# A new order of steps and buffers in an unrolled TensorE-bound kernel (decay attention, then a mixture of attention experts)

## The chip, the cores and the metric

The kernel runs on one core of one Trainium2 chip. The metric is the device time of one execution in microseconds (us). Engine names in the profile: PE is TensorE, PEld its weight loads, DVE is VectorE, ACT is ScalarE, POOL is GpSimd, SP is SyncE, which here only issues DMAs.

## What is computed

Two stages, cut from the reference. B = 4 batches, H = 8 heads, S = 768 tokens, D = 48; then E = 4 experts, Hd = 64, model width 384.

```python
def _attn_ref(r, k, v, w, u):
    state = np.zeros((B, H, D, D))
    for t in range(S):
        kt, vt, rt = k[:, :, t], v[:, :, t], r[:, :, t]
        cur = np.einsum('bhd,bhe->bhde', u[None] * kt, vt)
        y[:, :, t] = np.einsum('bhd,bhde->bhe', rt, state + cur)
        state = w[None, :, :, None] * state + np.einsum('bhd,bhe->bhde', kt, vt)

def _moe_ref(x, w_gate, wq, wk, wv, wo):          # x: (4, 768, 384), K = 2, scale = 1/8
    logits = x @ w_gate
    topk = np.argpartition(-logits, K, axis=-1)[..., :K]
    w = softmax of the two largest logits
    for e in range(E):
        q, k, v = x @ wq[e], x @ wk[e], x @ wv[e]
        a = softmax(causal(scale * (q @ k.transpose(0, 2, 1))))
        ye = a @ v @ wo[e]
        out += (gate weight of e, 0 where e is not in topk) * ye
```

## The kernel before

**The first stage** works on 24 chunks of 128 tokens (n = 0 to 23, six per batch). k and r of a chunk lie in rotating buffers `kdbuf` and `rdbuf` (four each), v in `vhbuf`, and a copy of v with its halves exchanged in `vsbuf`. The steps of a chunk: `load_chunk` and `load_vh` (DMAs on SP's queue), `load_vs`, `a_decay` (k and r times tables of powers of w; on DVE at L512 for the first chunks, on POOL at L514 for the others), `a_ku` (POOL, L521 and L523: the products for the u term), `a_own` (DVE, L530 and L532: their sum, times v), `a_transpose` (PE, L542: four transposes of k, four of r; copied out of PSUM by ACT into `kt`, L550, `rt`, L559, and `rx`, L563; chunk 0 by DVE, L548 and L556), `a_quarters` (PE, L579: scores inside 64 x 64 blocks, then the outer products of k and v, L587, called sums here), `a_mask` (DVE, L596, makes `sm`), `a_sum` (DVE, L635, and POOL, L639: the running state `z`), `a_out` (PE, L612 and L616), `a_add` (DVE, L623, twice: the chunk's x, in `ownv`), `a_xt` (PE, L646, transposes x; ACT, L649, copies its rounded part `xt_hi`) and `a_xl` (DVE, L656, the remainder `xt_lo`).

**The tables** are made once: a DMA brings w (`load_w`, L294 on ACT's queue), a transpose turns it (L297), `powers` builds the powers on DVE, `table` (L423, L425) expands them, L431 transposes them into the one buffer `psb` of two PSUM banks, and `table_out` (ACT, L435) copies them to `tab_k` and `tab_r`. The first `a_decay` steps on DVE read them in `psb`.

**The second stage** works on groups G of three chunks (eight groups, two per batch). Each weight is split in two numbers, hi and lo (`hi_qk` on ACT and `lo_qk` on DVE, L476, make `wqk_hi` and `wqk_lo`; `hi_v` and `lo_v`, L489 and L491, the same for `wv`), and each product is three matmuls. The steps: `m_proj` (PE, L687: q and k), `m_values` (PE, L722: v and the gate's logits), `m_gate` (DVE), `m_scores` (PE, L774 and L775, into `psb`; DVE, L781, mask and maximum; ACT, L783, exp), `m_weigh` (POOL, L796), `m_turn` (PE, L804: transposes; ACT, L808, copies them to `pt`), `m_av` (PE, L824) and `m_out` (PE, L847 to L849, then a copy and the DMA out). `warm_up` (L354) and `keep` (L393) are PE work without a result, put among the first steps.

**The order.** Every step is a generator that stops at places inside it. All of the program is unrolled from one table, ORDER, of 1629 words. A word names a step and its arguments and lets it run to its next stop; the digits behind "/" are the numbers of the rotating buffers that it takes there (PSUM: six of one bank, `ps`, and the one `psb`; in SBUF among others six `pr` and twelve `pt`). Each engine's and each DMA queue's instructions stand in the order in which the words issue them, and the framework puts a semaphore wait wherever an instruction needs another engine's or queue's. So a word that stands elsewhere moves everything that it issues, on every engine.

Of the kernel before, what the change touches and what calls it, by code (L numbers as in the profile page):

```python
# [21 lines left out]
a_decay,1,1 load_uw/2 warm_up a_quarters,0/34 a_quarters,0 a_transpose,1/0 a_mask,0/01 a_decay,2,1 load_uw load_vs,0
load_vs,0 a_transpose,0/0 a_ku,1/0 a_ku,1 a_ku,0/1 a_ku,0 lo_o,1 a_transpose,2/5 a_sum,0/0 a_transpose,1/1
a_transpose,2/0 a_transpose,1/1 load_vs,1 a_transpose,1/11 table_out,0 a_transpose,2/2 a_out,0 a_own,1/01 a_sum,0
a_own,0/0 a_quarters,1/5 a_transpose,2/22 a_sum,0/1 a_ku,2/0 a_decay,3,0 a_sum,1 a_add,0 a_sum,1/2 a_quarters,2/12
a_xt,0/3 keep,0/4 a_transpose,3/4 load_vs,2 hi_v load_vs,2 load_vs,1 a_transpose,3/1 a_xt,0/0 a_ku,2 load_chunk,4
load_qk,1/5 hi_qk,1 load_vh,3 load_chunk,4 load_chunk,5 a_mask,1/23 a_out,1 load_qk,0/2 load_vh,4 load_chunk,5
a_mask,2/01 a_sum,2 a_own,2/0 a_out,2 load_vh,6 load_chunk,6 load_chunk,6 load_vh,5 a_decay,3,1 a_decay,4,0 a_xl,0/0
a_ku,4/1 a_ku,3/0 a_sum,2/0 a_ku,3 a_decay,4,1 a_decay,5,0 a_decay,5,1 a_add,1 a_transpose,4/4 a_transpose,3/3
a_xt,1/0 a_transpose,4/0 a_transpose,3/00 a_xt,1 lo_v m_values,0,0/5 a_add,2 lo_qk,1 a_xl,1 a_xt,2/1 a_xt,2 make_lower  # L30
hi_qk,0 a_quarters,3/24 a_transpose,4/3 a_xl,2 lo_qk,0 m_values,0,0/0 m_proj,0,0,0/0 load_vs,3 a_transpose,4/11
m_proj,0,0,0/0 m_proj,0,0,0 m_proj,0,1,0/1 load_vs,3 m_proj,0,1,0/0 m_values,0,0/2 m_values,0,2/3 m_proj,0,0,1/0
a_sum,3 a_own,3/1 m_proj,0,1,0 m_proj,0,1,0 m_values,0,2 a_mask,3/23 m_proj,0,1,0 m_proj,0,0,1/1 m_proj,0,0,0/01
m_values,0,1/5 a_ku,5/0 a_sum,3/1 a_ku,5 a_decay,6,0 a_decay,6,1 make_sums,0 a_out,3 m_proj,0,0,1 m_values,0,1
m_gate,0/100 a_add,3 a_transpose,5/0 m_values,0,1 load_vs,5 m_values,0,2 a_transpose,5/1 a_transpose,5/5 m_gate,0
a_transpose,5/22 load_vs,5 m_scores,0,0,2/0 a_own,5/30 m_scores,0,0,2/01 a_quarters,4/12 a_xt,3/4 m_scores,0,0,1/0
a_transpose,6/0 a_sum,4 m_scores,0,0,1/10 a_xt,3/1 a_xl,3/1 a_transpose,6/0 hi_o,0 load_vs,4 m_scores,0,0,1
a_quarters,5/5 m_scores,0,0,0/0 load_chunk,8 load_chunk,7 load_chunk,9 m_proj,0,0,1/23 load_vs,6 load_vs,6 load_vh,7
a_mask,4/01 m_gate,0/400 m_proj,0,1,1/0 m_values,1,0/4 a_ku,6/0 a_ku,4 a_sum,4/2 m_scores,0,0,0/23 a_own,4/1
m_scores,0,1,2/0 m_scores,0,0,0 load_vs,4 m_scores,0,0,2 a_mask,5/23 a_sum,5 m_values,1,0/1 m_weigh,0,0/0  # L40
m_scores,0,1,2/35 a_decay,8,0 m_weigh,0,0 a_ku,6 a_out,4 a_add,4 m_values,1,0/1 m_proj,0,1,1 m_proj,0,1,1 a_out,5
a_add,5 a_xt,4/4 m_scores,0,1,0/0 m_scores,0,1,0/42 m_turn,0,0,0/1 m_scores,0,1,2 a_xt,4 a_xl,4 m_turn,0,0,2/2
a_xt,5/3 m_turn,0,0,0/0 a_xt,5 m_scores,0,1,1/0 m_scores,0,1,1/53 m_turn,0,0,2/1 a_transpose,6/5 m_turn,0,0,1/1
a_transpose,8/4 m_scores,0,2,1/0 m_scores,0,1,1 m_proj,0,1,1 a_transpose,6/00 m_scores,0,1,0 a_transpose,8/1 a_xl,5
m_proj,1,0,0/2 m_scores,0,2,1/10 m_proj,0,1,1 lo_o,0 m_scores,0,2,2/0 m_proj,1,1,0/3 m_weigh,0,1/1 m_scores,0,2,2/21
a_own,6/01 m_scores,0,3,1/0 m_scores,0,2,1 m_proj,1,0,0/0 m_proj,1,0,0 m_scores,0,3,1/04 m_proj,1,1,0 m_values,1,1/5
load_chunk,8 load_chunk,7 m_proj,1,0,0/01 load_vh,8 m_weigh,0,1 a_decay,8,1 m_values,1,1 m_turn,0,0,1/2 m_values,1,1
m_proj,1,1,0 m_turn,0,1,0/4 m_scores,0,3,2/0 m_scores,0,3,2/32 m_turn,0,1,1/2 a_quarters,6/1 m_scores,0,2,0/0
m_turn,0,1,1/3 m_scores,0,2,2 a_sum,6/0 m_proj,1,1,0 m_values,1,2/5 m_proj,1,0,1/2 m_scores,0,2,0/53 a_mask,6/01
m_proj,1,1,0 m_scores,0,2,0 m_scores,0,3,1 m_turn,0,1,0/4 a_sum,6 m_weigh,0,2/2 m_values,1,2 m_values,1,2  # L50
m_scores,0,3,2 m_gate,1/311 m_scores,0,3,0/0 m_turn,0,1,2/4 m_scores,0,3,0/45 m_turn,0,1,2/5 m_proj,1,0,1/1
m_scores,0,3,0 a_out,6 a_decay,7,0 a_decay,7,1 m_weigh,0,2 a_transpose,8/5 m_turn,0,2,0/4 m_scores,1,0,0/0 a_add,6
m_weigh,0,3/3 m_scores,1,0,0/13 m_gate,1 m_gate,1/311 m_proj,1,0,1 m_weigh,0,3 m_proj,1,1,1/0 a_transpose,8/11
m_turn,0,2,0/6 m_proj,1,1,1 m_scores,1,0,0 m_scores,1,1,2/0 m_turn,0,3,0/1 m_scores,1,1,2/25 m_turn,0,3,0/7
m_turn,0,3,1/5 a_xt,6/4 a_xt,6/0 m_turn,0,2,2/3 a_transpose,7/2 a_transpose,7/0 m_turn,0,3,1/8 a_transpose,7/1
a_xl,6/0 m_proj,1,1,1 m_scores,1,0,2/0 m_turn,0,2,2/9 a_transpose,7/22 m_turn,0,3,2/4 m_values,2,0/2 m_turn,0,2,1/5
m_turn,0,3,2/a m_turn,0,2,1/b m_scores,1,0,2/54 m_scores,1,0,1/0 m_scores,1,0,1/02 m_proj,1,1,1 m_proj,1,1,1
m_values,2,0/0 a_ku,8/1 a_ku,7/0 a_ku,7 a_sum,6/1 a_quarters,7/31 a_quarters,8/45 m_scores,1,1,0/0 a_sum,7
m_scores,1,0,2 m_scores,1,1,2 m_scores,1,0,1 m_values,2,0/0 a_own,7/0 a_mask,7/23 m_scores,1,1,0/30 a_ku,8 a_decay,9,0
a_sum,7/2 make_sums,1 a_sum,8 m_weigh,1,0/0 m_av,0,0,0,3/0 m_av,0,1,0,3/2 m_scores,1,1,0 m_av,0,0,0,3/0 m_av,0,1,0,3/1  # L60
m_scores,1,1,1/0 a_mask,8/01 m_scores,1,1,1/41 m_av,0,1,0,3/0 m_weigh,1,0 load_vh,10 load_vs,9 load_vs,8 load_vs,7
load_vs,9 m_proj,1,0,1/23 load_vs,7 a_out,7 a_add,7 load_vs,8 a_out,8 load_chunk,11 load_chunk,11 load_chunk,10
load_chunk,10 load_chunk,9 load_chunk,12 load_vs,10 load_vs,10 load_vs,11 load_chunk,12 load_vh,9 m_scores,1,1,1
m_weigh,1,1/1 m_weigh,1,1 m_av,0,0,0,3/1 a_decay,11,1 a_decay,10,0 a_decay,10,1 a_own,8/1 a_xt,7/2 m_turn,1,0,2/3
m_turn,1,0,4/1 m_turn,1,0,4/0 m_turn,1,0,2/4 a_add,8 m_scores,1,2,2/0 m_turn,1,0,1/0 m_out,0,1/1 a_xt,7 a_xl,7
a_xt,8/4 m_turn,1,0,5/3 m_turn,1,0,1/2 m_out,0,1/0 m_turn,1,0,0/5 m_turn,1,0,3/0 a_transpose,9/2 m_out,0,0/1
a_transpose,9/0 a_xt,8 m_turn,1,0,5/3 m_turn,1,1,2/2 m_turn,1,0,0/1 m_turn,1,1,2/5 m_turn,1,0,3/6 m_scores,1,2,2/13
m_scores,1,3,0/0 a_decay,9,1 a_ku,9/0 a_ku,9 m_turn,1,1,1/3 a_transpose,10/5 a_transpose,10/1 a_transpose,10/2
m_scores,1,3,0/52 a_xl,8 m_scores,1,2,1/0 m_turn,1,1,4/0 m_turn,1,1,1/7 m_turn,1,1,4/8 m_out,0,0/1 m_turn,1,1,3/4
m_turn,1,1,5/5 a_transpose,9/3 m_turn,1,1,0/0 m_turn,1,1,5/b a_transpose,9/00 m_turn,1,1,3/9 a_transpose,10/22  # L70
m_scores,1,2,1/24 m_scores,1,3,2/0 a_own,9/10 m_scores,1,3,2/00 m_proj,2,0,0/5 m_scores,1,3,1/0 a_quarters,9/3
# [838 lines left out]
```

## Time and profile before

| | before |
|---|---|
| times of three runs | 325.73, 325.08, 325.06 us, median 325.08 |
| profiled execution: span | 323.2 us |
| around the span (median less span) | 1.9 us |
| PE, PEld busy | 317.0 us (98%), 280.8 us (87%) |
| DVE, ACT, POOL busy | 215.7 (67%), 228.5 (71%), 173.9 us (54%) |
| DMA | 37.35 MB, mean 116 GB/s |

The profiled execution's own time is not listed apart from its span; the three runs are other executions of the same program. The span is that of the one core; busy shares are of the span. In the views below a row such as "L579 <- ACT rt L559" says that an instruction of line 579 waited for the one of line 559 on ACT; "issue" is time in which an engine waited for nothing that the profile shows.

### The profile page before, as it was taken

The page shows a single profiled execution, that of the slowest core. Times are in us where ns is not written, and L with a number is a line of the kernel's source. Part 1 is how long each engine was busy: PE and PEld are TensorE (multiplying, and loading weights), DVE is VectorE, ACT ScalarE, POOL GpSimd, SP SyncE. Part 2 cuts the span into 40 slices and gives each one's busy share as a digit, 9 for nine tenths or more (in the row PEclk, how much of TensorE's full clock was granted, in tenths as well). Part 3 has the DMA queues.
Part 4 walks back from the last instruction along what each step waited for, and adds up shares of the span by engine and source line. Part 5 has one row for each costly group of instructions (what it writes and reads, how often), then busy time and mean ns, then how long its engine had stood idle before and what let it go on. Part 6 is the DMA issues. An engine that isn't in the chain of part 4 may idle for free.

```text
span 323.2 us, 11932 instructions
## 1 busy us (share of the span) xinstructions
PE 317.0 (98%) x4815; PEld 280.8 (87%) x4815; DVE 215.7 (67%) x693; ACT 228.5 (71%) x605; POOL 173.9 (54%) x227
## 2 busy tenths in 40 slices
...
PEclk9999999999999999999999999999999999999999
...
GB/s 175 193 213 135 102 202 84 145 174 165 62 75 203 106 116 108 184 103 96 175 99 124 147 127 49 178 218 64 4 51 54 216 28 2 124 122 32 44 26 99
DMA packets 104695, 37.35 MB, mean 116 GB/s; under 512 B 95550, under 2 KB 100544, under 8 KB 104640
## 3 DMA queue, kind: packets, MB, share of 16 engines
...
q8 instruction: 38, 0.62, 0.8%
q14 instruction: 17, 0.14, 0.1%
...
## 4 chain that ended last, share of the span: by engine, by line
PE 78%; POOL 6%; DVE 3%; ACT 2%; issue 2%; DMA 1%; SPq 0%; POOLq 0%; DVEq 0%
PE ps L687 13%; PE ps L804 11%; PE ps L824 10%; PE ps L722 8%; PE psb L774 6%; PE psb L775 5%; PE ps L542 4%; PE ps L616 3%; PE ps L579 3%; PE ps L612 3%; PE ps L847 2%; POOL pr L796 2%; PE ps L849 2%; PE ps L848 2%; PE ps L587 2%; PE ps L646 2%
## 5 line engine op out<-in xcount | busy, mean ns | idle before, releaser
L796 POOL TENSOR_SCALAR pr<-pr,f,gate 128x128 f32<-128x128 f32 (+5 forms) x96 | 67.8, 722 | 98.4 <-DVE f L790 57.8
L781 DVE CUSTOM_DVE_ANT_0 pr<-psb,after 128x512 f32<-128x512 f32 (+5 forms) x96 | 59.6, 621 | 53.1 <-PE psb L775 37.9
L808 ACT ACTIVATE pt<-ps 128x384 f32<-128x384 f32 (+2 forms) x143 | 55.1, 423 | 22.5 <-PE ps L804 20.6
L783 ACT ACTIVATE pr<-pr,nm 128x512 f32<-128x512 f32 (+5 forms) x96 | 63.7, 666 | 10.2 <-DVE nm L781 9.8
L804 PE MATMUL ps<-ident,pr 128*128 128x128 f32 x336 | 51.2, 274 | 0.0
L774 PE MATMUL psb<-tk,tq 128*128 128x384 f32 (+3 forms) x128 | 46.7, 365 | 0.0
L804 PEld LDWEIGHTS ps<-ident,pr 128*128 128x128 f32 x336 | 39.6, 141 | 3.7 <-issue 1.3
L775 PE MATMUL psb<-tk,tq 128*128 128x384 f32 (+3 forms) x128 | 40.6, 323 | 0.0
L824 PE MATMUL ps<-pt,vv 128*64 128x384 f32 (+2 forms) x322 | 39.9, 393 | 0.0
L824 PEld LDWEIGHTS ps<-pt,vv 128*64 128x64 f32 x322 | 20.9, 136 | 17.5 <-issue 13.4
L687 PE MATMUL ps<-xt_hi,wqk_hi 128*128 128x384 f32 x96 | 33.4, 348 | 0.0
L687 PE MATMUL ps<-xt_hi,wqk_lo 128*128 128x384 f32 x96 | 32.4, 337 | 0.0
L687 PE MATMUL ps<-xt_lo,wqk_hi 128*128 128x384 f32 x96 | 32.3, 337 | 0.0
L521 POOL TENSOR_TENSOR ku<-kdbuf,uw 128x384 f32<-128x384 f32 x24 | 25.2, 1055 | 9.6 <-DVE ps L530 9.2
L514 POOL TENSOR_TENSOR rdbuf<-rdbuf,tab_r 128x384 f32<-128x384 f32 x22 | 23.9, 1090 | 5.8 <-DMA rdbuf<-in_r_dram 5.4
L774 PEld LDWEIGHTS psb<-tk,tq 128*128 128x128 f32 x128 | 24.2, 189 | 2.1 <-DVE nm L781 0.7
L697 ACT ACTIVATE tk<-ps 64x384 fp32r<-64x384 f32 x32 | 15.4, 484 | 13.4 <-PE ps L687 8.3
L523 POOL TENSOR_TENSOR ku<-ku,rdbuf 128x384 f32<-128x384 f32 x24 | 24.2, 1012 | 0.7
L775 PEld LDWEIGHTS psb<-tk,tq 128*128 128x128 f32 x128 | 24.3, 190 | 0.0
L612 PE MATMUL ps<-vhbuf,sm 64*64 64x48 f32 x384 | 24.0, 219 | 0.0
L612 PE MATMUL ps<-vsbuf,sm 64*64 64x48 f32 x384 | 23.6, 219 | 0.0
L514 POOL TENSOR_TENSOR kdbuf<-kdbuf,tab_k 128x384 f32<-128x384 f32 x21 | 21.5, 1024 | 1.1 <-DVE ex L755 1.1
...
## 6 DMA issues: line engine op xcount, KB each, us to landing
...
```

The lines of the kernel that those rows point to most:

```text
L514: nc.gpsimd.tensor_tensor(t[:, :, :D], t[:, :, :D], (tab_k, tab_r)[which], op=OP.mult)
L612: nc.tensor.matmul(o, st["sm", n][par][rows, p // 2, i], values, start=fresh, stop=True)
L687: nc.tensor.matmul(ps, a[:, t, m0:m0 + P], x[:, t, :], start=i == 0, stop=i == n - 1)
L722: nc.tensor.matmul(ps, x[:, t, cols], a[:, t, :], start=m == 0, stop=m == n - 1)
L774: nc.tensor.matmul(o, tq[:, 0, q], keys[:, n0:n1], start=True, stop=False)
L775: nc.tensor.matmul(o, tq[:, 1, q], keys[:, n0:n1], start=False, stop=True)
L781: nc.vector.tensor_tensor_reduce(pr[:, :N], ps, after[:, S - N:], 1.0, 3e38, op0=OP.add, op1=OP.min, accum_out=nm)
L783: nc.scalar.activation(pr[:, :N], pr[:, :N], AF.Exp, bias=nm, scale=-1.0, accum_out=sums[:, e, j, 0:1])
L796: nc.gpsimd.tensor_scalar(p[:, :N], p[:, :N], f[:, i], gate[:, i, e:e + 1], op0=OP.mult, op1=OP.mult)
L804: nc.tensor.transpose(pst[:, j, :], mg[G]["p", e, j][:, i * C:(i + 1) * C], ident)
L808: nc.scalar.activation(pt[:, j0:], pst[:, j0:], AF.Copy)
L824: nc.tensor.matmul(psy[par * HD:par * HD + HD, j0 * C:j1 * C], vv[:, i % GC, e, :], mg[G]["t", e, i][:, j0:j1].rearrange("s j t -> s (j t) ...
```

## The change

Only the table ORDER is written anew: the same 1629 words in another order, with other buffer numbers behind the "/". It is said to come from a search that counts TensorE's instruction pages (the blocks in which an engine's instructions are fetched). No step's code differs, and every engine and queue issues the same instructions as before. The table has four lines fewer, so every line number behind it is lower by 4 after the change (L512 becomes L508). Its first line:

```diff
 ORDER = """
-make_ident load_w/0 load_o,1/0 make_lower pad,0 pad,4 warm_up/1 keep,2/0 warm_up/1 warm_up warm_up load_w load_chunk,1
...
+load_w/0 load_uw load_w make_ident keep,2/5 pad,0 load_chunk,0 make_before make_lower make_ones warm_up/3 warm_up/1
...
```

The table is rewritten throughout; four places follow, as rows of an engine's program, before and after (the number behind a name's "_" only keeps buffers apart).

ACT's first instructions, before. `ownv0<-in_w` is the load of w for the tables, `row<-in_w` and `row<-in_u` are the row loads of `load_uw`:

```order
L294 DMA ownv0_100<-in_w_dram 4x2x48
L442 DMA row_171<-in_w_dram 1x384
L443 DMA row_171<-in_u_dram 1x384
L498 ACT_TABLE_LOAD
L498 ACTIVATE wo_hi_177<-pr0_70 128x384
L425 ACTIVATE vv0_121<-pr2_72 128x4x64
```

And after:

```order
L438 DMA row_171<-in_w_dram 1x384
L439 DMA row_171<-in_u_dram 1x384
L290 DMA ownv0_100<-in_w_dram 4x2x48
L421 ACT_TABLE_LOAD
L421 ACTIVATE vv0_121<-pr0_70 128x4x64
```

The two row loads now stand ahead of the load of w, and the rounding of half of wo has left this place.

DVE where the tables are used, before. `psb0` holds the tables, `ps3` and `ps4` the scores of chunk 0:

```order
L512 TENSOR_TENSOR kdbuf0_148<-kdbuf0_148,psb0_69 128x8x48
L512 TENSOR_TENSOR kdbuf1_149<-kdbuf1_149,psb0_69 128x8x48
L512 TENSOR_TENSOR kdbuf2_150<-kdbuf2_150,psb0_69 128x8x48
L512 TENSOR_TENSOR rdbuf1_153<-rdbuf1_153,psb0_69 128x8x48
L596 TENSOR_TENSOR sm0_110<-ps3_66,before_164 128x256
L596 TENSOR_TENSOR sm1_111<-ps4_67,before_164 128x256
```

And after:

```order
L508 TENSOR_TENSOR kdbuf1_149<-kdbuf1_149,psb0_69 128x8x48
L508 TENSOR_TENSOR kdbuf0_148<-kdbuf0_148,psb0_69 128x8x48
L508 TENSOR_TENSOR rdbuf1_153<-rdbuf1_153,psb0_69 128x8x48
L592 TENSOR_TENSOR sm3_113<-ps0_63,before_164 128x256
L592 TENSOR_TENSOR sm0_110<-ps5_68,before_164 128x256
L508 TENSOR_TENSOR kdbuf2_150<-kdbuf2_150,psb0_69 128x8x48
L508 TENSOR_TENSOR rdbuf2_154<-rdbuf2_154,psb0_69 128x8x48
```

k of chunk 1 now stands ahead of k of chunk 0, and both buffers of chunk 2 behind the mask of chunk 0.

PE behind the sums of chunk 0 (L587), before: the transposes of k (`kdbuf`) and r (`rdbuf`) of chunks 1 and 2, then a_out of chunk 0 and the quarters of chunk 1:

```order
L587 MATMUL ps4_67<-vhbuf0_156,kdbuf0_148 64x48
L542 MATMUL ps0_63<-ident_163,kdbuf1_149 128x128 x4
L542 MATMUL ps5_68<-ident_163,kdbuf2_150 128x128 x4
L542 MATMUL ps1_64<-ident_163,rdbuf1_153 128x128 x4
L542 MATMUL ps2_65<-ident_163,rdbuf2_154 128x128 x4
L616 MATMUL ps4_67<-z0_114,rt0_104 64x48
...
L579 MATMUL ps0_63<-rt1_105,kt1_103 64x64
```

And after:

```order
L583 MATMUL ps5_68<-vhbuf0_156,kdbuf0_148 64x48
L538 MATMUL ps2_65<-ident_163,kdbuf1_149 128x128 x4
L538 MATMUL ps4_67<-ident_163,rdbuf1_153 128x128 x4
L612 MATMUL ps5_68<-z1_115,rt1_105 64x48
...
L350 MATMUL ps1_64<-pr3_73 128x512
L389 MATMUL ps3_66<-ident_163 128x128 x4
L575 MATMUL ps2_65<-rt0_104,kt0_102 64x64
```

The transposes of chunk 2 have left this place; they now stand behind those of chunk 0's x and directly ahead of chunk 2's own quarters. A warm-up matmul and a `keep` stand ahead of chunk 1's quarters.

DVE shortly before the first `m_proj`, before. `wqk_lo` is the remainder of half of wq and wk, `ownv0` the x of chunk 2, `xt_lo0` that of chunks 1 and 2, transposed:

```order
L623 TENSOR_TENSOR ownv0_100<-ps1_64,ownv0_100 128x2x2x48
L623 TENSOR_TENSOR ownv0_100<-ps2_65,ownv0_100 128x2x96
L476 TENSOR_TENSOR wqk_lo_174<-pr5_75,wqk_hi_173 128x4x3x64
L656 TENSOR_TENSOR xt_lo0_126<-ps0_63,xt_hi0_124 128x3x128
L656 TENSOR_TENSOR xt_lo0_126<-ps1_64,xt_hi0_124 128x3x128
L476 TENSOR_TENSOR wqk_lo_174<-pr2_72,wqk_hi_173 128x4x3x64
```

And after:

```order
L472 TENSOR_TENSOR wqk_lo_174<-pr5_75,wqk_hi_173 128x4x3x64
L619 TENSOR_TENSOR ownv1_101<-ps5_68,ownv1_101 128x2x2x48
L619 TENSOR_TENSOR ownv1_101<-ps3_66,ownv1_101 128x2x96
L652 TENSOR_TENSOR xt_lo1_127<-ps4_67,xt_hi0_124 128x3x128
L472 TENSOR_TENSOR wqk_lo_174<-pr1_71,wqk_hi_173 128x4x3x64
L652 TENSOR_TENSOR xt_lo1_127<-ps2_65,xt_hi0_124 128x3x128
```

The first `wqk_lo` moved ahead of the additions that make the x of chunk 2, and the second ahead of that chunk's `xt_lo`.

More of the change, by code (lines that the diff above doesn't have):

```diff
@@ L22 @@
[L22 to L71, printed above, removed]
@@ L87 @@
-m_values,2,1 a_quarters,11/43 a_quarters,12/02 m_scores,2,1,2/42 a_mask,11/23 a_sum,11 a_mask,12/01 a_own,11/0
-m_turn,1,3,0/3 m_scores,2,0,0 m_turn,1,3,1/b m_scores,2,1,2 a_sum,12/0 m_gate,2/500 m_av,1,1,0,3/1 m_av,1,1,3,6
-m_gate,2 m_av,1,1,3,6/1 m_scores,2,0,2 a_out,11 m_gate,2/500 a_add,11 m_av,1,1,3,6/0 a_out,12 a_transpose,14/5
-a_transpose,13/4 a_transpose,14/0 m_scores,2,1,0/0 a_transpose,14/3 a_xt,11/1 a_own,12/1 m_weigh,2,0/0 a_add,12
-a_transpose,13/1 a_xt,11 a_xl,11 m_scores,2,1,0/21 load_chunk,16 m_proj,2,0,1/32 load_vs,14 load_vs,13 load_chunk,15
@@ new lines @@
+table,1 load_vh,0 powers load_vs,0 load_vs,0 table_out,0 load_chunk,1 a_decay,1,0 table_out,1 a_decay,0,1 load_chunk,1
+load_uw/3 load_uw a_quarters,0/05 a_decay,0,0 a_transpose,0/0 a_quarters,0 a_decay,1,1 a_ku,0/0 make_sums,0 a_ku,0
+a_mask,0/30 a_sum,0/1 a_transpose,1/2 load_chunk,2 a_decay,2,0 a_transpose,1/0 a_transpose,1/4 a_transpose,1/01 a_ku,1/1
+a_ku,1 a_out,0 load_chunk,2 a_decay,2,1 load_vh,1 warm_up keep,0/3 a_own,0/1 a_sum,0 a_quarters,1/21 a_add,0 load_vs,1
+a_mask,1/01 load_v/4 load_vh,2 a_sum,0/0 a_sum,1 a_xt,0/4 a_transpose,2/3 hi_v a_own,1/0 a_transpose,2/1 a_transpose,2/0
@@ new lines @@
+a_transpose,2/22 a_quarters,2/53 load_chunk,3 load_vs,1 lo_v a_out,1 a_xt,0/0 a_xl,0/1 a_sum,1/1 a_decay,3,0
+a_transpose,3/0 a_ku,2/0 a_ku,2 load_vs,2 a_transpose,3/0 load_qk,1/5 hi_qk,1 load_chunk,4 a_add,1 a_xt,1/4 a_xt,1
+a_decay,4,0 load_vs,2 load_chunk,3 a_mask,2/01 a_decay,3,1 m_values,0,0/1 a_sum,2 a_transpose,4/2 a_transpose,4/1
+load_qk,0/1 load_chunk,4 a_decay,4,1 a_own,2/1 a_out,2 load_vh,3 load_chunk,5 load_o,1/2 a_transpose,3/0 lo_qk,1 hi_qk,0
+a_add,2 a_xt,2/2 a_transpose,3/01 a_quarters,3/53 load_chunk,5 a_xl,1 a_xt,2 load_vh,5 a_ku,3/0 a_ku,3 lo_qk,0
@@ new lines @@
+a_quarters,4/25 m_scores,0,0,2/32 m_values,0,0 a_transpose,5/22 a_own,5/31 a_mask,4/13 a_xt,3/0 a_xt,3/1
+m_scores,0,0,1/0 a_transpose,6/1 m_scores,0,0,1/00 a_quarters,5/4 a_transpose,6/0 load_chunk,6 a_ku,4/0 a_ku,4 a_xl,3/0
+m_scores,0,0,2 m_values,1,0/0 m_scores,0,0,1 a_sum,4 a_sum,4/1 load_vs,4 m_gate,0 a_own,4/0 m_scores,0,0,0/0 a_sum,5
+m_values,1,0/1 m_proj,0,1,1/1 m_values,1,0/1 load_o,0/3 hi_o,0 load_vh,7 a_mask,5/02 a_decay,6,1 load_vs,5
+m_scores,0,0,0/24 m_scores,0,0,0 a_ku,6/1 a_ku,6 load_vs,5 m_gate,0/010 m_weigh,0,0/2 m_weigh,0,0 m_scores,0,1,2/0
@@ new lines @@
+m_turn,1,3,0/5 m_scores,2,1,0/0 load_chunk,13 a_decay,13,1 a_transpose,11/00 a_quarters,11/4 m_values,2,2 a_ku,13
+m_turn,1,3,1/7 a_quarters,12/30 a_decay,14,1 m_gate,2/501 m_scores,2,0,0 m_av,1,1,0,3/5 a_sum,11 a_mask,11/21
+m_values,2,1 m_gate,2 m_gate,2/110 m_scores,2,1,2 a_sum,12/1 a_own,12/0 a_mask,12/30 a_sum,12 m_scores,2,1,0/41
+m_av,1,1,3,6 a_decay,14,0 m_av,1,1,3,6/1 m_av,1,1,3,6/1 a_out,11 a_add,11 load_vs,12 a_out,12 a_transpose,14/2
+load_vh,13 m_scores,2,0,1 m_scores,2,0,2 m_weigh,2,0/0 m_weigh,2,0 a_transpose,14/1 a_xt,11/1 a_xt,11 m_scores,2,1,1/0
@@ new lines @@
+m_out,1,2/5 a_sum,12/2 m_out,1,2/0 load_chunk,15 load_chunk,15 m_scores,2,1,1/02 m_scores,2,2,2/0 m_turn,2,0,0/4
+a_transpose,13/2 a_decay,15,0 m_scores,2,1,1 a_transpose,13/0 a_transpose,13/5 a_decay,15,1 a_xl,11 a_add,12 a_xt,12/1
+a_xt,12/0 a_xl,12/1 m_scores,2,1,0 m_out,1,2 m_out,1,0/0 a_own,13/30 a_transpose,13/22 m_weigh,2,1/2 m_out,1,0/0
+m_weigh,2,1 m_proj,3,0,0/2 a_transpose,14/1 m_proj,3,0,0/1 a_transpose,14/00 m_values,3,0/5 m_values,3,0/0
+a_quarters,13/0 m_turn,2,1,0/1 m_turn,2,0,0/8 m_values,3,0/0 load_vs,15 m_scores,2,2,2/30 m_proj,3,0,0 a_sum,13
```

308 lines of the change are left out of this document (167 added, 141 removed).

## The prediction

> **What bounds the kernel now.** I read the page first (engines, the row of the granted clock, the chain, the queues), then the table of stages, then the waits of two stretches, then the timeline of the first 30 us.
>
> ```profile
> span 323.2 us, 11932 instructions
> PE 317.0 (98%) x4815; PEld 280.8 (87%) x4815; DVE 215.7 (67%) x693; ACT 228.5 (71%) x605; POOL 173.9 (54%) x227
> PEclk9999999999999999999999999999999999999999
> q8 instruction: 38, 0.62, 0.8%
> PE 78%; POOL 6%; DVE 3%; ACT 2%; issue 2%; DMA 1%; SPq 0%; POOLq 0%; DVEq 0%
> ```
>
> PE is busy for 98% of the span at the full granted clock, and holds 78% of the chain that ended last; the other engines have a third of their time free. The queue q8 made 38 fetches of 0.62/38 MB, 16 KB each. PE has 2 x 4815 = 9630 records, so 253 per fetch: these are TensorE's instruction pages.
>
> ```profile
> core 0: us, PE busy (x) PEld busy (x) DVE busy (x) ACT busy (x) POOL busy (x), PEclk, DMA share, GB/s
> 0.00:28.40 28.40, 25.52 (x527) 19.90 (x528) 22.33 (x59) 17.39 (x38) 21.95 (x36) 1.00 0.88 191
> 28.40:60.00 31.60, 31.60 (x540) 29.81 (x539) 26.46 (x89) 22.98 (x62) 17.31 (x22) 1.00 0.61 135
> 240.00:300.00 60.00, 60.00 (x628) 52.99 (x627) 38.57 (x131) 44.86 (x124) 18.89 (x27) 1.00 0.32 80
> 300.00:323.20 23.20, 20.16 (x168) 15.93 (x166) 5.21 (x17) 13.82 (x38) 5.21 (x6) 0.97 0.15 53
> ```
>
> At 28.40 the first m_proj starts. From there to 300 us PE is never without work; before it, DVE is busy 22.3 of 28.4 us and the DMA engines 88%. An order can win or lose in three places: the head, small waits behind it, and the tail. The waits of PE's weight loads, first for 0 to 28.4, then for 28.4 to 300:
>
> ```profile
> PEld ps L579 <- ACT rx L563: 0.6, 1, 0.6
> PEld ps L722 <- DVE wv_lo L491: 0.5, 1, 0.5
> PEld ps L579 <- ACT rt L559: 0.4, 1, 0.4
> ...
> PEld ps L824 <- issue: 11.9, 66, 0.2
> PEld ps L579 <- issue: 1.4, 5, 0.4
> PEld ps L616 <- DVE sm L596: 0.7, 2, 0.4
> ```
>
> The head waits for ACT and DVE. Behind it only 0.7 us for one reason is a wait for another engine; the 11.9 us before L824 are 0.18 us at each pair of its matmuls, whatever the order.
>
> **The pages.** Counted in PE's order of before, a page ends inside the sums of chunk 1, 256 instructions on inside a_out of chunk 1, and 256 on inside a_quarters of chunk 3. At each the weight loads, else 7 ns apart, have a hole:
>
> ```profile
> 21.00 0.41 PEld L612 LDWEIGHTS ps<-vhbuf,sm 64*64 64x64 f32 x3
> ...
> 26.39 0.50 PE L579 MATMUL ps<-rt,kt 64*64 64x64 f32 x17
> 27.13 0.40 PE L579 MATMUL ps<-rt,kt 64*64 64x64 f32 x12 [0.23 <-issue]
> ```
>
> Three loads take 0.41 us where one takes 0.14, so 0.2 us is lost; at 27.13 the starts are about 0.4 us late with nothing to wait for. The first of the three is about 0.1. That is 0.7 us in all; at the ends of later pages I find nothing over 0.1 us. So 0.7 us (0.2%) is the most that freeing PE of page ends can give, and all of it lies ahead of 28.4. [...]
>
> **The change, part by part.** No instruction is added or taken away on DVE, POOL or in PE's matmuls, only waits and places differ. What the pages gain is contained in the times compared below, so it is not subtracted twice. I walk the head of the changed order with durations of before:
>
> ```profile
> 3.94 0.18 PEld L297 LDWEIGHTS ps<-ident,ownv 4*128 4x128 f32 x1 [0.88 <-DMA ownv<-in_w_dram]
> 2.38 0.29 ACTq L442 DMA_DIRECT2D row<-in_w_dram  x1
> 10.12 0.49 ACT L435 ACTIVATE tab_r<-psb 128x384 f32<-128x384 f32 x1 [3.17 <-PE psb L431]
> 10.64 1.48 DVE L512 TENSOR_TENSOR kdbuf<-kdbuf,psb 128x384 f32<-128x384 f32 x3 [1.14 <-DMA kdbuf<-in_k_dram]
> 11.69 0.63 PE L587 MATMUL ps<-vhbuf,kdbuf 64*64 64x48 f32 x32
> 10.69 1.01 POOL L514 TENSOR_TENSOR rdbuf<-rdbuf,tab_r 128x384 f32<-128x384 f32 x1 [0.37 <-ACT tab_r L435]
> 12.89 1.00 POOL L523 TENSOR_TENSOR ku<-ku,rdbuf 128x384 f32<-128x384 f32 x1
> 16.89 0.55 DVE L532 TENSOR_TENSOR ownv<-vhbuf,ps 128x384 f32<-128x384 f32 x1
> 18.12 0.61 DVE L623 TENSOR_TENSOR ownv<-ps,ownv 128x192 f32<-128x192 f32 x2
> 16.50 0.59 ACT L559 ACTIVATE rt<-ps 128x512 f32<-128x512 f32 x1
> 22.74 1.20 DVE L489 TENSOR_TENSOR wv_lo<-pr,wv_hi 128x768 fp32r<-128x768 f32 x1
> 25.28 1.77 DVE L476 TENSOR_TENSOR wqk_lo<-pr,wqk_hi 128x768 fp32r<-128x768 f32 x1
> 26.97 1.01 DVE L656 TENSOR_TENSOR xt_lo<-ps,xt_hi 128x384 fp32r<-128x384 f32 x2
> 27.90 1.82 DVE L476 TENSOR_TENSOR wqk_lo<-pr,wqk_hi 128x768 fp32r<-128x768 f32 x1
> 28.40 0.42 PE L687 MATMUL ps<-xt_hi,wqk_hi 128*128 128x384 f32 x1
> ```
>
> - The load of w that L297 waits for (0.88 idle) stands third on ACT's queue instead of first, behind two row loads of about 0.29: +0.3, so the tables stand in PSUM at 10.3 instead of 10.0. If the 1.25 us of the first load were the price of being first, 0; so 0 to +0.3.
> - Reads of psb by ACT and DVE wait for each other. Now they alternate: ACT tab_k, DVE kdbuf1, ACT tab_r, DVE kdbuf0, at 0.5 each from 10.4: kdbuf0 is ready at 12.5 and chunk 0's sums start at 12.6, not 11.69. Cost 0.9; one warm-up matmul that left this place gives nothing back, for PE waits here.
> - rdbuf0 on POOL follows tab_r: three POOL operations of 1.0 from 12.0 end at 15.0. DVE then needs L530 (0.55), L532 (0.55), one z and the two additions (0.61), so x of chunk 0 is there at 17.1, where a_xt 0 stands. In before that happened at 19.0, but with chunk 2's quarters already made.
> - Chunk 2's two groups of transposes come now directly ahead of its quarters. They end at 18.35; ACT must copy rt (0.59) first: quarters at 19.15, PE idle 0.8. In before ACT's copies of chunk 2 had several us, and PE still waited 0.4 and 0.6 there.
> - Quarters, sums and a_out 1 take 2.1, to 21.3; the additions (0.61) let a_xt 1 start at 22.0; m_values, a transpose group and a_out 2 end at 25.1, one more group at 25.55.
> - DVE has the first wqk_lo (1.77, from 24.4) ahead of the additions of chunk 2: x at 26.7, PE idle 1.2. Chunk 3's quarters, sums and a transpose group bring the first m_proj to 28.65.
> - Its second matmul reads xt_lo of chunk 2, which now stands behind the second wqk_lo: 26.7 + 0.5 + 1.8 + 0.5 = 29.45, while PE is there at 28.8. PE idle 0.65. In before both xt_lo stood ahead of that subtraction.
>
> So the second matmul of m_proj starts at 29.4 instead of 28.6: **+0.8**. Bounds: if both wqk_lo took the 1.20 of wv_lo, which has the same shape, 1.2 goes away (-0.4); another stall like the 0.96 us of L491 (12 columns) on this DVE chain adds up to +0.9 (+1.7). I take +0.8, because POOL runs beside both wqk_lo here as it did when they took 1.8.
>
> Behind 28.4 the same steps follow in nearly the same places; SP's loads keep their lead on their users. Banks of ps are reused by a transpose or quarter step a little sooner (nearest 0.45 us of PE work after the last writer, where 0.76 was nearest), which an ACT copy of 0.5 can turn into a wait of 0.2 to 0.3, at two or three places; against that, before's waits of 0.7 for sm may go. I take **0**, bounds -0.6 and +0.8.
>
> The tail:
>
> ```profile
> 251.66 3.38 PE ps L824 x24
> 305.06 2.09 PE ps L824 x12
> 308.61 1.45 PE ps L824 x12
> 310.68 1.64 ACT L808 ACTIVATE pt<-ps 128x384 f32<-128x384 f32 x4
> ```
>
> The last m_av over all heads' first half was split, with transposes between (2.09 and 1.45); now it is one block of 3.38, and eight groups of three transposes run together. ACT copies one group in 1.64/4 = 0.41, PE makes one in 0.33, so after eight ACT is 0.66 behind; five shorter transposes (0.5) cover most: **+0.2**, bounds -0.1 and +0.6.
>
> Sum: 0.8 + 0 + 0.2 = +1.0. The profiled execution has a span of 323.2; the median of the runs is 325.08, so 1.9 lies around the span, and I leave that as it is: 324.2 of span, 326.1 of time. A run of this kernel differs from another by up to 0.2% (0.65 us), so less than that is "no change".
>
> **The rivals.**
> - Faster, 324.4. The subtraction wqk_lo decides: if it takes 1.2 where it now stands, neither a_xt 2 nor the second matmul of m_proj waits for it, and the walk is 1.2 shorter: -0.4; with the load of w not late, -0.7. For it: the row of L489. Against it: both rows of L476, and that POOL's work beside it stays. It decides below about 1.25 us for each.
> [...]
> - Slower still, 326.9. Behind 28.4 the sooner reuse of banks costs 0.3 at three places. For it: distances of 0.45. Against it: PE's queue has other work ahead at most of them.
>
> **How the numbers follow.** The slower head alone has 0.33 and with more waits behind it 0.12, so 0.45 for slower; no change 0.28; faster 0.27, because a new order of all steps may also take away waits that I priced at nothing. The likeliest gives 326.1 (its own range 325.7 to 327.7). For eight in ten I go from 323.7, the faster rival less the 0.7 us of waits for sm behind 28.4, to 327.7, the head and tail at their bounds together (0.8 + 0.9 + 0.6 = 2.3 over 325.08, and a little of the waits behind).
>
> **What would show it.** In the changed profile, PE's sums of chunk 0 start near 12.6; the waits of 0 to 30 us name ACT rt for L575, and DVE for a_xt and L683; the first m_proj has a hole after its first matmul; the tables alternate between ACT and DVE; the loads at page ends have no holes. The prediction is wrong if m_proj's second matmul starts before 28.6, which would mean a shorter DVE chain, or if PE waits over 1 us between 30 and 300 us.

## The result, and the profile after

The changed kernel takes 329.52 us (median of 4 runs, 328.87 to 331.35) against 325.35 (325.06 to 325.73): ratio 1.0142, 95% interval 1.0112 to 1.0172, 4.2 us slower. The direction was forecast, the size (+1.0, range to 327.7) was not. The page of the profiled execution after (329.29 us), its engines, its instruction queue and its chain:

```profile
span 327.4 us, 11945 instructions
PE 317.1 (97%) x4814; PEld 280.4 (86%) x4815; DVE 217.1 (66%) x693; ACT 229.5 (70%) x605; POOL 174.0 (53%) x227
q8 instruction: 38, 0.62, 0.8%
PE 91%; DVE 5%; ACT 1%; issue 1%; DMA 1%; DVEq 0%
```

The table of stages after, cut at the times that were used for before (stretch, length, busy time of PE, PEld, DVE, ACT and POOL, granted clock, DMA share, GB/s):

```profile
0.00:28.40 28.40, 23.14 (x458) 18.02 (x459) 20.97 (x57) 15.37 (x32) 19.05 (x34) 1.00 0.86 182
28.40:60.00 31.60, 30.23 (x550) 27.71 (x553) 26.82 (x81) 22.49 (x63) 20.40 (x24) 1.00 0.57 127
...
240.00:300.00 60.00, 60.00 (x626) 52.98 (x626) 36.91 (x128) 44.77 (x125) 21.66 (x31) 1.00 0.36 90
300.00:327.40 27.40, 23.89 (x199) 19.50 (x195) 7.83 (x23) 16.37 (x44) 7.61 (x9) 1.00 0.13 45
```

PE does the same 317 us of work. (The page counts 13 instructions more than before's. The work of the engines is the same, one record of PE is missing, and the others are waits on semaphores, of which the new order needs more; so "the same instructions" holds for the work alone.) It is idle 2.4 us longer up to 28.4 (23.14 busy instead of 25.52), 1.4 us longer from there to 60, and 0.5 longer behind 300 (3.5 instead of 3.0): together the 4.2 us. The waits of PE's weight loads after, up to 36 us (instruction, what it waited for, sum in us, count, mean):

```profile
PEld ps L293 <- DMA ownv<-in_w_dram: 1.7, 1, 1.7
...
PEld ps L575 <- ACT rt L555: 1.0, 1, 1.0
PEld ps L583 <- DVE kdbuf L508: 1.0, 1, 1.0
...
PEld ps L683 <- DVE xt_lo L652: 0.4, 1, 0.4
```

And from 28.4 to 300 us, where the largest waits of before for another engine are 0.7 for sm in two and 0.5 for nm in three:

```profile
...
PEld ps L575 <- ACT pt L804: 1.0, 2, 0.8
...
PEld ps L538 <- DVE xq L700: 0.7, 1, 0.7
PEld ps L612 <- DVE z L631: 0.6, 1, 0.6
PEld psb L770 <- DVE nm L777: 0.6, 1, 0.6
```

The last three rows of the first fence are waits that the prediction named. Its first is a wait of a size that the prediction did not give, and the rows of the second are places that it did not see. PE itself waits 1.2 us for other engines in this stretch (0.5 for a sum, L528, on DVE ahead of L575, 0.4 for xq, 0.3 for nm), in before 0.2. Two costs stand in none of these rows: the speed of PE ahead of 10 us, and the ends of instruction pages.

### The profile page after: what moved, and what is told of

Read it like the earlier page. It is cut to its first block, busy times and chain, and to the rows that moved or that the text cites. A ratio compares the mean times of both kernels' runs of the same rounds, so it can differ in the third digit from the quotient of the medians.

```text
span 327.4 us, 11945 instructions
## 1 busy us (share of the span) xinstructions
PE 317.1 (97%) x4814; PEld 280.4 (86%) x4815; DVE 217.1 (66%) x693; ACT 229.5 (70%) x605; POOL 174.0 (53%) x227
## 4 chain that ended last, share of the span: by engine, by line
PE 91%; DVE 5%; ACT 1%; issue 1%; DMA 1%; DVEq 0%
PE ps L683 15%; PE ps L820 12%; PE ps L800 11%; PE ps L718 7%; PE psb L770 7%; PE psb L771 6%; PE ps L538 6%; PE ps L575 4%; PE ps L608 4%; PE ps L612 4%; PE ps L583 3%; PE ps L843 3%; PE ps L845 3%; PE ps L844 3%; PE ps L642 3%
## 5 line engine op out<-in xcount | busy, mean ns | idle before, releaser
L777 DVE CUSTOM_DVE_ANT_0 pr<-psb,after 128x512 f32<-128x512 f32 (+5 forms) x96 | 59.6, 621 | 49.4 <-PE psb L771 31.3
L779 ACT ACTIVATE pr<-pr,nm 128x768 f32<-128x768 f32 (+5 forms) x96 | 63.7, 667 | 10.7 <-DVE nm L777 10.4
L770 PE MATMUL psb<-tk,tq 128*128 128x384 f32 (+3 forms) x128 | 46.5, 363 | 0.3 <-DVE nm L777 0.3
L770 PEld LDWEIGHTS psb<-tk,tq 128*128 128x128 f32 x128 | 24.3, 189 | 2.1 <-DVE nm L777 0.6
L510 POOL TENSOR_TENSOR rdbuf<-rdbuf,tab_r 128x384 f32<-128x384 f32 x22 | 22.4, 1025 | 5.7 <-ACT tab_r L431 3.4
```

Source lines behind the costliest of these rows:

```text
L510: nc.gpsimd.tensor_tensor(t[:, :, :D], t[:, :, :D], (tab_k, tab_r)[which], op=OP.mult)
L770: nc.tensor.matmul(o, tq[:, 0, q], keys[:, n0:n1], start=True, stop=False)
L777: nc.vector.tensor_tensor_reduce(pr[:, :N], ps, after[:, S - N:], 1.0, 3e38, op0=OP.add, op1=OP.min, accum_out=nm)
L779: nc.scalar.activation(pr[:, :N], pr[:, :N], AF.Exp, bias=nm, scale=-1.0, accum_out=sums[:, e, j, 0:1])
```

## The experiments

Every kernel has all words of ORDER and computes everything; only their order differs, with buffers as in the kernel that they come from. In all, 16 kernels were timed, each beside the kernel before on the same chip (its medians there: 325.40 for x, 325.02 for y, 325.12 for z, 325.32 for q and p). The times of one kernel with the changed head lie 0.5 to 2.5 us apart, and an interval is about 0.5 us to each side; so a difference of two such kernels below 1 us says little by itself, and is used only where a trace shows the same thing. The last two columns are of the one profiled execution of each kernel: the time (us from the start of the span) at which the first m_proj starts, and the time from there to the end. By its first m_proj PE has done the same 526 or 527 instructions in all of them.

```
                                   median   ratio to before, interval   first m_proj   behind it
before                             325.35                             28.40         294.8
after                              329.52   1.0142 (1.0112 to 1.0172)   30.02         297.4
x1 head after, rest before         328.84   1.0111 (1.0094 to 1.0128)   32.03         295.8
x2 head before, rest after         326.28   1.0034 (1.0021 to 1.0046)   28.42         296.5
x3 after to 75 us, then before     330.53   1.0159 (1.0138 to 1.0179)   30.68         297.7
x4 after, tail before              329.49   1.0124 (1.0107 to 1.0141)   31.09         297.1
y1 after, load of w first          327.98   1.0100 (1.0084 to 1.0115)   28.87         297.1
y2 after, keep 1 ahead             328.48   1.0106 (1.0092 to 1.0120)   29.39         296.9
y3 after, two DVE steps moved      328.45   1.0119 (1.0097 to 1.0141)   30.82         297.0
y4 = y1 + y3                       327.81   1.0089 (1.0076 to 1.0103)   29.68         296.3
z1 = y4 + loads later              327.27   1.0072 (1.0059 to 1.0084)   28.66         296.7
z4 = y4 + k of chunk 0 first       327.15   1.0060 (1.0046 to 1.0074)   29.11         296.6
q1 = z1 + z4                       327.11   1.0048 (1.0035 to 1.0061)   29.07         296.3
q2 = q1 + a_out 1 ahead            327.50   1.0067 (1.0054 to 1.0079)   28.29         296.1
z2 before, load of w late          326.44   1.0039 (1.0026 to 1.0053)   30.11         294.8
z3 before, wo's loads late         325.58   1.0015 (1.0006 to 1.0024)   27.85         295.9
p1 before, tab_k later             325.37   1.0005 (0.9996 to 1.0013)   28.50         295.1
p2 = p1 + four loads later         325.48   1.0008 (1.0000 to 1.0016)   28.23         295.2
```

**Where the time went (x1 to x4).** Each takes the words of one order up to a cut and then those that are left in the other's order.

> The changed order up to its first m_proj, then the words that are left in the order of before; buffers as in the order that each word comes from. Theory W (waits): the 4.2 us are waits of PE at places that can be named, 1.6 of them ahead of the second matmul of m_proj, 1.9 between 31 and 80 us, 0.4 in the tail. It expects 325.35 + 1.6 = 327.0 us. Rival H (the head decides all, because everything behind starts late): 329.5. Rival P (instruction pages cost evenly along the program): about 325.7.

> The other way round: before up to its first m_proj, then the words that are left in the changed order. Theory W: 329.5 - 1.6 = 327.9 us. Rival H: 325.4. Rival P: 329.2.

> The changed order up to the first m_av (about 75 us), then before. Theory W: head and the waits up to 75 us, 325.35 + 1.6 + 1.6 = 328.6 us, and the trace shows the three waits at about 39, 58 and 64 us again. Rival H: 329.5. Rival P: a quarter of 4.2, so 326.4.

> The changed order up to the first word of m_scores 7,2 (about 298 us), then the order of before for the tail. Theory W: 329.5 - 0.4 = 329.1 us. Rival H: 329.5. Rival P: 329.2.

The changed head costs 3.4 us (328.84 against 325.40), the changed rest 0.9 (326.28), and 3.4 + 0.9 is the whole of 4.2 within the noise. That is twice what W gave the head. H is wrong too, since the rest costs 0.9 behind the head of before. The tail costs nothing that these runs can tell (329.49 without it against 329.52, though the ratios, 1.0124 and 1.0142, leave room for 0.6). x3 came out 1.9 above W; part of that is a wait at its seam (0.98 of PE's weight loads, 0.74 of PE itself, for ACT's copy vv, L727, ending at 79.05 us), and it was not followed further.

These are prices of two parts of the order, in medians; they do not say at which places the time is lost. In after's profile the first m_proj starts only 1.6 us later than in before's, and 2.6 more come behind it. The five profiles whose head has the words of after unchanged (after, x1, x3, x4, y3) start it at 30.02 to 32.03, the latest being x1, with a hole of 1.46 that is shown below.

The traces show a first reason why the head was mis-sized. PE's first instructions, from the timelines (start, duration, engine, line, tiles, count, idle time ahead), of before:

```profile
6.32 1.06 PE L542 MATMUL ps<-ident,kdbuf 128*128 128x128 f32 x4
8.17 0.60 PE L542 MATMUL ps<-ident,rdbuf 128*128 128x128 f32 x4
```

Of after:

```profile
4.57 0.27 PE L293 MATMUL ps<-ident,ownv 4*128 4x4 f32 x1 [0.75 <-DMA ownv<-in_w_dram]
6.95 1.06 PE L538 MATMUL ps<-ident,kdbuf 128*128 128x128 f32 x4
8.75 0.60 PE L538 MATMUL ps<-ident,rdbuf 128*128 128x128 f32 x4
```

Of x4, which begins with the same words as after:

```profile
9.09 1.06 PE L542 MATMUL ps<-ident,rdbuf 128*128 128x128 f32 x4
9.95 0.89 PE L393 MATMUL ps<-ident 128*128 128x128 f32 x4
10.68 1.04 PE L431 MATMUL psb<-ident,vv 128*128 128x128 f32 x8
```

Four transposes take 1.06 us at first and 0.60 later: PE starts at little more than half its speed and steps up once. The granted clock is 1.00 in every stretch of 2 us from the start to 12 us (before and after), so it does not show the step, which is read off these durations. In before the step comes ahead of 8.17, in x4 only behind 9.95. In after PE stands idle 0.75 us until w has landed, and in the six profiles with such an idle time the step (the start of the first faster instruction) lies between 8.2 and 10.4 us; in the twelve without, between 4.8 and 7.6. What sets the moment of the step within these bounds was not shown.

**The step to full speed (y1, y2, z2).**

```diff
y1  -load_w load_uw load_w make_ident
    +load_w load_w load_uw make_ident
y2  -load_w/0 keep,1/4 warm_up warm_up
    +keep,1/4 load_w/0 warm_up warm_up
z2  (before)  load_uw moved ahead of the second load_w
```

> The changed order with one word moved: the load of w for the tables stands first on ACT's queue again, ahead of the two row loads. In the profiles so far TensorE's first instructions run at half speed (a 128x512 warm-up matmul 0.63 us, later 0.38), and the step to full speed comes at 7.7 us in before, but between 8.4 and 10.4 us wherever the changed head runs, in which PE stands idle for 0.75 us until w has landed. Theory C (the idle time also puts off the clock's step): w lands at 3.9, PE does not stand idle, the step comes before 8 us again: 0.75 for the load and 0.4 to 1.3 for the clock, 329.5 - 1.6 = 327.9 us, with less spread. Rival W (only the load's own lateness counts): 328.8. Rival N (the late load is covered): 329.5.

> The changed order with one filler moved: the four transposes of keep 1 stand ahead of the transpose of w instead of behind it, so PE has work while it waits; the load stays late. Theory C: the step of the clock comes before 8 us, and 0.4 to 1.3 us are won: 328.7 us. Rival W: nothing is won, 329.5 to 329.6.

> The kernel before with one word moved: the two row loads stand ahead of the load of w on ACT's queue, as in the changed order. Theory C: w lands 0.6 to 0.8 later, PE stands idle, the clock's step comes at 8.3 us or later instead of 7.7: 325.0 + 1.2 = 326.2 us, with more spread. Rival W (the load's lateness alone): 325.7. Rival N: 325.0.

y1 wins 1.5 us and y2 1.0 (1.4 and 1.2 by the ratios), and z2 loses 1.3 in the kernel before: three times theory C. In y2 w is as late as in after (L293 starts at 4.61; in after at 4.57, in y1 at 3.75), and only PE's idle time is filled. So the idle time and what follows from it are worth about 1.0; the further 0.5 of y1, which would be the load's own lateness, is within the noise. What the 0.75 us of idle time cost by themselves, and what the slower speed behind them costs, the times do not separate. The traces show that both are there: the step is at 8.23 in after, 7.34 in y2 and 6.99 in y1, and the transposes of the tables start at 9.62, 8.69 and 8.55. In z2 PE idles 1.02 us and its first m_proj starts 1.7 later than in before. PE in the timeline of y2, where nothing idles ahead of the first row and the transposes are at full speed by 7.82:

```profile
4.61 0.26 PE L293 MATMUL ps<-ident,ownv 4*128 4x4 f32 x1
7.82 0.60 PE L538 MATMUL ps<-ident,rdbuf 128*128 128x128 f32 x4
```

**DVE behind the head (y3, y4).**

```diff
-m_proj,1,0,0 lo_o,0 load_vs,6
+m_proj,1,0,0 load_vs,6          (lo_o,0 now ahead of m_weigh,0,1)
-m_gate,0/201 m_values,0,2 ... m_proj,0,0,1/0 m_proj,0,0,1
+m_values,0,2 ... m_proj,0,0,1/0 m_proj,0,0,1 m_gate,0/201
```

> The changed order with two DVE steps moved behind the head: the remainder of the second half of wo (1.48 us beside POOL's work at 56 us, 0.56 in before) goes ahead of the weights of expert 1, where POOL is idle; and the gate of group 0 goes behind the subtraction that frees a bank for the transposes of chunk 6. Theory W: the waits of PE at 58 to 60 us (1.2) and at 39 us (0.56) go: 329.5 - 1.8 = 327.7 us. Rival S (slack: what is won there is lost at the next wait): 329.0 or more.

> Both: the load of w first, and the two DVE steps moved. Theory C with W: 329.5 - 1.6 - 1.8 = 326.1 us. Rival (head and middle are not additive): 327 or more.

y3 wins 1.1 of the 1.8 by the medians and 0.7 by the ratios (its times go from 328.16 to 330.01), so its size is not settled; what its two moves do can be read in the traces. The remainder of wo in the timeline of before:

```profile
51.30 0.56 DVE L501 TENSOR_TENSOR wo_lo<-pr,wo_hi 128x384 fp32r<-128x384 f32 x1
```

The same in the timeline of after, below POOL's row of that time and above two waits of PE (in brackets):

```profile
55.39 2.01 POOL L510 TENSOR_TENSOR kdbuf<-kdbuf,tab_k 128x384 f32<-128x384 f32 x2
...
56.33 1.48 DVE L497 TENSOR_TENSOR wo_lo<-pr,wo_hi 128x384 fp32r<-128x384 f32 x1
...
58.45 0.19 PEld L770 LDWEIGHTS psb<-tk,tq 128*128 128x128 f32 x1 [0.55 <-DVE nm L777]
...
59.60 0.69 PE L575 MATMUL ps<-rt,kt 64*64 64x64 f32 x32 [0.53 <-DVE ownv L528]
```

The same instruction takes 0.56 where POOL is idle and 1.48 beside POOL's products. The score's maximum (L777) and a sum (L526, L528) stand behind it on DVE, and PE waits for both. In y3 it takes 0.55, as its timeline shows; the wait of L770 is gone and the one ahead of L575 is 0.2:

```profile
54.03 0.55 DVE L497 TENSOR_TENSOR wo_lo<-pr,wo_hi 128x384 fp32r<-128x384 f32 x1
```

The other move only changed the name of the wait. L538 no longer waits for the subtraction L700, which still read the PSUM bank that the transposes of chunk 5 take (the expectation says chunk 6), but the quarters behind it (L575) now wait for the gate, whose results lie in the PSUM bank that they take; PE's waits in y3:

```profile
PEld ps L575 <- DVE dl L742: 0.9, 1, 0.9
```

y4 is only 0.2 below y1, although its moves lie behind the head. In the profiles they win 0.8 there (296.3 behind the first m_proj instead of 297.1), and the first m_proj starts 0.8 later, with a new hole of about 1.1 in the head, at the end of a page.

**The pages.** In three timelines there are holes in the middle of a dense step, with no releaser ("issue" in the brackets). In x1, among the sums of a chunk:

```profile
19.42 0.33 PE L587 MATMUL ps<-vhbuf,kdbuf 64*64 64x48 f32 x9 [1.28 <-issue]
```

In y4, among the weight loads of an a_out:

```profile
21.73 0.14 PEld L608 LDWEIGHTS ps<-vsbuf,sm 64*64 64x64 f32 x2 [1.03 <-issue]
```

And in p2 at the same kind of place:

```profile
21.66 0.13 PEld L612 LDWEIGHTS ps<-vhbuf,sm 64*64 64x64 f32 x1 [1.17 <-issue]
```

Counted in PE's order, each lies at a page end (in before the holes at 16.46, 21.28 and 27.13 are 256 instructions apart), and the fetches are in the DMA records (38 of 16 KB in before). Over the 666 page ends of the 18 profiles PE never entered a page sooner than 1.25 us after the end of its fetch; some 35 page ends lie between 1.25 and 1.55, and nearly all the holes are among them. A fetch starts between 2.6 us before PE enters the page ahead of it and 5.2 us after; at page ends 2 to 4, in the head, it is 0.65 to 3.6 us after. Every delay of more than 2.4 us falls in a stretch in which the DMA engines are 80% busy or more, but early fetches are found in such stretches too: that the loads hold the fetch up is argued, not shown.

```
fetch starts after entry into the page ahead (us) / hole (us) at page ends 2, 3, 4
before  2.2 / 0.10    2.4 / 0.20    3.4 / 0.41
after   1.3 / 0       2.7 / 0.49    2.0 / 0
x1      2.4 / 1.46    2.2 / 0.39    1.2 / 0
y4      0.8 / 0       3.3 / 1.09    1.8 / 0
z1      1.2 / 0       1.7 / 0       2.0 / 0
p2      1.9 / 0       3.4 / 1.28    2.3 / 0
```

So the holes of before were not removed. They moved, and their size changes from profile to profile.

```diff
z1  load_qk,0 moved behind load_chunk,5; load_o,1 moved behind load_vh,5
z3  (before)  load_o,1 moved behind a_out,2; hi_o,1 lo_o,1 load_o,0 moved behind the first m_proj
z4  a_decay,0,0 moved ahead of table_out,0
```

> The kernel with both edits (load of w first, two DVE steps moved; 327.8), and two loads on SP's queue moved: the load of wk (384 KB) from ahead of chunk 4's r to behind chunk 5's k, that of half of wo to behind v of chunk 5. Theory D: a page of TensorE's instructions can be fetched only when PE has left the page before the last, and the fetch then queues behind the data loads under way; PE enters a page no sooner than 1.25 to 1.5 us after its fetch ends. With fewer loads under way at 16 us the fetch starts within about 1 us instead of 3.3, the hole inside a_out of chunk 1 (1.1 in that kernel's profile) goes, and 0.4 to 1.1 are won: 327.1 us. Rival (the fetch's delay has nothing to do with the loads): 327.8.

> The kernel before with the loads of wo's two halves (192 KB each, first and eighth among SP's loads), their rounding and the first remainder moved behind the head. Theory D: k and r land about 1 us sooner, DVE's wait of 1.1 for k goes, and the page fetches of the head find fewer loads ahead: the three holes of 0.14, 0.24 and 0.45 shrink: 324.4 us. Rival (the waits for ACT's copies behind them take it back): 325.0.

> The kernel with both edits (327.8), and k of chunk 0 multiplied first on DVE, ahead of the copies of the tables and of k of chunk 1. The prediction's second step: PE's wait of 1.0 ahead of the sums of chunk 0 goes, 0.7 is won: 327.1 us. Rival (x of chunk 0 hangs on POOL's three operations and not on these sums, or a page's hole takes it back): 327.6.

z1 is 0.5 below y4: the fetch starts 1.7 us after PE's entry instead of 3.3, and the hole of 1.1 is gone, as D has it. But one profile does not show that the moved loads did it: in y1, whose head is that of y4 and in which no load was moved, the delay is 1.8 and there is no hole either. The first part of theory D, that a fetch waits until PE has left the page before the last, does not hold: 204 of the 666 fetches start before PE enters the page ahead. z4 is 0.7 below y4, and where that comes from is open. The sums of chunk 0 start 0.95 sooner (10.76 instead of 11.71), but the transpose of chunk 0's x starts at 17.02 instead of 16.79, and chunk 2's quarters at 19.21 instead of 18.99. The sum that x of chunk 0 needs (L526) now waits for POOL's third product, the rival that its expectation names; in y4 and in z4:

```profile
14.70 0.56 DVE L526 TENSOR_REDUCE ps<-ku 128x8 f32<-128x384 f32 x1 [0.51 <-PE ps L608]
...
14.93 0.56 DVE L526 TENSOR_REDUCE ps<-ku 128x8 f32<-128x384 f32 x1 [1.05 <-POOL ku L519]
```

z4's profile gets ahead of y4's only at page end 3, whose hole is 0.64 instead of 1.09. z3 went wrong: it is 0.5 slower than before. Its first m_proj comes sooner (27.85 against 28.40), yet the loads that were moved now lie ahead of the fourth page's fetch, whose hole grew from 0.41 to 0.76, and what was left of the gain went in a wait for nm at 39 us (0.30) and in the hole of a page end at 133 us (about 0.3).

**What adds up (q1, q2, p1, p2).**

```diff
q2  -a_transpose,2 a_quarters,2 load_chunk,3 load_vs,1 lo_v a_out,1
    +a_transpose,2 a_out,1 a_quarters,2 load_chunk,3 lo_v   (load_vs,1 behind hi_v)
p1  (before)  table_out,0 moved behind the last a_transpose,2
p2  (before)  p1, and load_vh,6 load_chunk,6 (twice) load_o,0 moved behind m_proj,0,0,0
```

> The changed order with all edits so far (load of w first, two DVE steps moved, two loads later, k of chunk 0 first on DVE). If the parts add up: 327.8 - 0.5 - 0.7 = 326.6 us. Rival (the last two win the same time, since the page's hole is there in one and not in the other): 327.1.

> The kernel with all these edits, and a_out of chunk 1 (with the copy of v that it needs) ahead of the quarters of chunk 2, so that PE has work while ACT copies chunk 2's transposes: the prediction's wait of 0.8 there goes. 326.6 - 0.7 = 325.9 us. Rival P (PE only comes sooner to the end of the page, which lies inside a_out or just behind it, and waits there): 326.5.

> The kernel before with ACT's copy of the table for k behind its copies of chunk 2's transposes, for which PE waits 0.37 and 0.61 there. rt and rx end 0.4 sooner, POOL's product for chunk 3 starts 0.4 later, which has slack: 325.1 - 0.35 = 324.75 us. Rival P (the next page end gives it back): 325.1.

> The same, and four loads that the head does not need (half of wo, and k, r and v of chunk 6) moved behind the first m_proj, 768 KB less ahead of the page fetches between 12 and 27 us. Theory D: the holes at the three page ends (0.14, 0.24, 0.45) go: 324.35 us. Rival (other loads take their place ahead of the fetches): 324.75.

q1 is no faster than z1 or z4 alone by the medians, as the rival has it; by the ratios it is 0.4 to 0.8 us faster, so this is not settled. In q2 the wait of 1.0 for rt is gone, and another of the same size stands in its place, for the running state that a_out needs (first fence: PE's waits in q2 from 14 to 30 us). Yet its first m_proj starts at 28.29, as early as before's (28.40), in the one profile, which is of its fastest run; what that run loses to before lies behind, 296.1 instead of 294.8. p1 is no faster than before: the wait for rt is gone, and the one for the 12 columns of wv's remainder is 0.9 instead of 0.5, and PE, which comes there sooner, waits 0.6 for POOL's r (second fence: the view of p1 from 15 to 29 us). In p2 two holes went and one of 1.28 came. No kernel tried beats the one before.

```profile
PEld ps L612 <- POOL z L635: 1.1, 1, 1.1
```

In p1:

```profile
PEld ps L722 <- DVE wv_lo L491: 0.9, 1, 0.9
...
PEld ps L542 <- POOL rdbuf L514: 0.6, 1, 0.6
```

## Why the prediction was right or wrong

- *The load of w, +0.3 (bounds 0 to +0.3).* **This is the step that failed most.** It measured 1.5 (y1), in before 1.3 (z2). The load was taken by its lateness alone, and that was too small too: two row loads of 0.29 are 0.6, and the transpose of w started 0.63 later (4.57 instead of 3.94). The 0.75 us in which PE then had nothing to do put its step to full speed at 8.2 to 10.4 us instead of 4.8 to 7.6, and the transposes, the tables and all behind them came later. The row of 0.88 idle for PEld ahead of L297 was read as a wait of PE, but PE itself had no gap there.
- *kdbuf0 behind kdbuf1, +0.9.* Right in place and wait (sums at 12.9, forecast 12.6; a wait of 1.0). ACT and DVE do take turns at psb in after (starts 10.69, 11.22, 11.81 and 12.33; the last three stood idle 1.08, 0.62 and 0.56, each until the one ahead had ended). But taking the wait away (z4) brought x of chunk 0 no sooner, for POOL's third product then was the last to come.
- *The walk behind it.* x of chunk 0 was forecast for 17.1 and came at 18.0, quarters of chunk 2 at 19.15 and 20.2. The addition was late since the sum L526, which writes into a PSUM bank on which a_out was still at work, started about 0.5 late, and POOL's third product ended at 15.5, not 15.0. PE's wait for rt was 0.74 as forecast 0.8, but covering it (q2) won nothing by the medians.
- *The first wqk_lo, 1.77 as in before.* It took 1.38, the second 1.79.
- *The second wqk_lo ahead of xt_lo.* Forecast +0.65 ahead of the second matmul of m_proj, measured 0.38; the matmul started at 30.56 instead of 29.4.
- *The head's sum of +0.8.* 3.4 by the medians (x1); in after's profile the second matmul of m_proj starts 1.9 later than in before's (30.56, 28.66). Of it 1.5 are the load of w with the step to full speed. After's profile also has a page's hole of 0.49. The rest was not separated.
- *Behind 28.4, 0 (bounds -0.6 to +0.8).* **The second step that failed:** 0.9 by the medians (x2), and in the profiles 1.7 (x2) and 2.6 (after) behind the first m_proj. PE's 1.2 us of waits between 30 and 300 us are over the 1 us that the prediction names as a sign of being wrong. Its reading of before was too short here as well: beside the 0.7 for sm, before's view has 0.5 for nm, 0.4 for z and 0.4 for dl. What the traces show is one DVE step that moved beside POOL's work (0.9 us longer, PE waiting behind it) and a wait of the transposes of chunk 5. That one is a reuse of a bank, as bounded, but for a reader that came late because a gate stood ahead of it on DVE, and not for a copy on ACT. The moves of both are worth about 0.7 (y3 by its ratios; the profiles of after, y1 and y2 have 296.9 to 297.4 behind the first m_proj, those of y4, z1, z4, q1 and q2 296.1 to 296.7). What the other 1.3 to 1.9 us against before's 294.8 are was not found. The prediction had used that very contention in the head (1.2 or 1.8 for one shape) and did not look for it elsewhere.
- *The tail, +0.2.* About 0 (x4), inside its bounds.
- *The pages, at most 0.7, all in the head.* The size in before was right. That freeing them can only win was not: a later page can have a hole (0.34 at 64 us in after), and a hole can be more than three times the largest of before (1.46, 0.41).
- *The rivals.* No change and faster were wrong. "Slower still" had its time from the reuse of banks; its side was right, its cause was so at one place at most.

Over the 18 profiles nearly all of the page ends with more than 1.55 us from the end of the fetch to PE's entry have no hole; a few at 62 to 65 us have holes of up to about 0.5. In this head the holes go up to 1.46 (x1).
